# Five weight narrowings that share their exponent work with ScalarE, and two instead of three projections in the first three steps

## The chip, the core and the metric

One NeuronCore of a Trainium2 chip runs the whole kernel in one launch. The metric is the device time of one execution in microseconds. Eight executions of the kernel before took 1217.54 to 1219.71 us, with a median of 1218.54 us.

## The reference

```python
X = np.fft.fft(x, axis=1)               # x: 8 x 3136 x 256, float32
X = np.fft.fft(X, axis=2)
y = X.real.astype(np.float32)
h = np.maximum(y @ w_in, 0.0)           # w_in: 256 x 1024
conv_out = sum(conv_w[k] * hp[:, k:k + S, :] for k in range(3))   # hp: h padded by one row on each side
gate = 1.0 / (1.0 + np.exp(-conv_out))
return (h * gate @ w_out).astype(np.float32)                      # w_out: 1024 x 256
```

The real part of a two-dimensional Fourier transform is projected from 256 to 1024 features and rectified. A convolution with three taps along the sequence gives the gate, and the gated h is projected back to 256 features. The three weights arrive as float64, so the kernel has to make float32 of them itself.

## The kernel before

**Transform.** The sequence transform is folded: VectorE (DVE) adds and subtracts mirrored rows of x (`fold_ops`, lines 158 to 187), TensorE (PE) multiplies the folded rows with cosine and sine tables (`units`), and the results are two tables per batch, `pt` (cosine part) and `qt` (sine part), with 128 features by 1569 frequencies. The feature transform is not applied to the data: TensorE multiplies it into w_in once (`blocks`, line 595), which gives G, so that `pt` and `qt` are projected to the 1024 features directly.

**Steps.** The main loop runs over 256 steps (b, c, f): 8 batches, 4 chunks c of some 386 frequencies, 8 groups f of 128 features. A chunk stands for frequencies k and their mirror images, so a step makes two halves of h from the same products: the front half is pa + pb and the back half is pa - pb, each then rectified, where pa is the product with `pt` and pb that with `qt`. Each step goes through these stages, in functions of the same names:

- `seed`: ScalarE (ACT) fills the PSUM bank pa with a rank-one term (line 641). For the first four steps (`first`) there is no seed, and `products` adds a one-row matmul, `pa<-er,left`.
- `products`: TensorE writes pb from `qt` and adds the product with `pt` to pa. In the steps that `triple` picks (here the first 20), it adds the product with `qt` to pa once more, so that pa holds the sum.
- `copies`: in a triple step ScalarE copies -2 pb to SBUF as nb (line 670) and rectifies the front half of h straight out of pa (line 672). In any other step it copies pb twice, once for each half (line 675).
- `combine`: VectorE makes the halves of h that are left, max(pa + nb, 0), with one custom instruction each (line 686): one in a triple step, two in any other.
- `first_tap` (ScalarE, line 692), `other_taps` (VectorE, two instructions at line 698), `sigmoid` (ScalarE, two halves, line 711), `gate` (GpSimd line 718 and VectorE line 719, half each), and `mm2`: TensorE multiplies g with w_out, 6 matmuls of 256 columns in most steps, and the finished tiles go through ScalarE to SBUF and by DMA to HBM.

**Narrowing.** A float64 weight is loaded as pairs of 32-bit words (`raw`, low word and high word). `narrow` makes float32 of a block of 512 values per partition with seven VectorE instructions: take the exponent bits (515), subtract 896 and clamp at zero (516), shift left by 23 (517), add the sign bit (518), mask the mantissa (520), join it with the low word (521), multiply by the power of two (522). In the loop there are five narrowings of this size: the last quarter of w_in in step 0, and the quarters of w_out in steps 2, 3, 5 and 7. The raw words of w_out lie in a buffer that the second half of the next batch's x takes over afterwards.

**Order.** The order on every engine is that of the program text, written by hand. Work beside the steps is put into `side` with `at(cycle, where, fn)`, and cycle t of the loop runs:

```python
if 0 <= t - 2 < n: sigmoid(steps[t - 2])
if t + 1 < n:
    products(steps[t + 1]); copies(steps[t + 1])
run("act")
if t < n: combine(steps[t])
run("dve")
...                                # seed of t + 2, first_tap of t, other_taps of t - 1, gate of t - 2
run("load")
if t >= LAG: mm2(steps[t - LAG])   # LAG is 3
run("pe")
```

At the end of cycles 0, 1 and 2, "pe" runs `blocks(1)`, `blocks(2)` and `blocks(3)`, which make the parts of G, together with `column`, which makes the seed's factors ge (ScalarE copies them, lines 595, 600 and 609). PSUM has two banks for pa, one for pb, one for `pd` and four for po. The tile `left` holds the factors of the one-row matmul in one row of its features 0 to 3, and from the last chunk of a batch on it holds leftover rows of the gated h.

Of the kernel before, what the change touches and what calls it, by code (L numbers as in the profile page):

```python
# [9 lines left out]
F32 = mybir.dt.float32  # L10
I32 = mybir.dt.int32
U32 = mybir.dt.uint32
AF = mybir.ActivationFunctionType
ALU = mybir.AluOpType
# [12 lines left out]

TRIPLE = 20  # L30
FIRST = 4
RC = 56
NQ = 8
# [5 lines left out]
def kernel(  # L39
# [10 lines left out]
    nc = tc.nc  # L50
    B, S, D = x.shape
    F = moe_w_in.shape[1]
    P = 128
# [9 lines left out]
    NF = F // P  # L63
# [6 lines left out]
    const = ctx.enter_context(tc.tile_pool(name="const", bufs=1))  # L70
# [19 lines left out]
    stt = nc.vector.scalar_tensor_tensor  # L90
    act = nc.scalar.activation

    def mm(o, l, r, start, stop):
        nc.tensor.matmul(o, l, r, start=start, stop=stop, skip_group_check=True)  # L94
# [12 lines left out]
    sg = const.tile([P, 2, 2], F32, name="sg")  # L107
# [3 lines left out]
    def load_ops(b, h, eng, other=None, held=False):  # L111


        def plain():
            t = xp.tile([P, 8, 2, D], F32, name="xh", tag="xh")
            xh[b, h] = t
            if held:

                nc.gpsimd.memset(t[0:1, 0, 0, 0:1], 0.0)
            eng.dma_start(out=t[0:NP, 0:4], in_=bass.AP(  # L120
                tensor=x.tensor, offset=x.offset + (b * S + 1 + 2 * h) * D,
                ap=[[HQ * D, NP], [Q4 * D, 4], [1, 2 * D]]))

        def zero():
            t = xh[b, h]
            for s0, n, r in ((0, 4, 0), (4, 3, 1), (7, 1, 0)):
                (other or eng).dma_start(out=t[NP:KR, s0:s0 + n], in_=bass.AP(
                    tensor=x.tensor, offset=x.offset + (b * S + r * Q4) * D,
                    ap=[[D, 1], [Q4 * D, n], [0, 2], [1, D]]))

        def mirrored(m):
            def f():
                nc.gpsimd.indirect_dma_start(  # L133
                    out=xh[b, h][0:NP, 7 - m].rearrange("p q d -> p (q d)"),
                    out_offset=None,
                    in_=bass.AP(tensor=x.tensor, offset=x.offset,
                                ap=[[2 * D, B * S // 2], [1, 2 * D]]),
                    in_offset=bass.IndirectOffsetOnAxis(ap=idx[0:NP, 0:1], axis=0),
                    element_offset=(b * S + (4 - m) * Q4 - HO + 2 * (1 - h)) * D)
            return f  # L140
        return [plain] + [zero] * h + [mirrored(m) for m in range(4)]
# [63 lines left out]
    PQ, eb, er = {}, {}, {}  # L205
    ed = edp.tile([B, (RC // 2 + 1) * RC], F32, name="ed")

    def table(k, st, q, cols):
        return tabs[st // 2][0:k, st, q, cols] if st < 2 else tabs[1][0:k, st - 2, q, cols]
# [55 lines left out]
    def product(o, w, st, q, cols, start, stop):  # L265

        def f(p):
            k = KR if q == HQ - 1 else NP
            mm(p[o], w(k, q), table(k, st, q, cols), start, stop)
        return f  # L270
# [232 lines left out]
    left = const.tile([P, NF, P], F32, name="left")  # L503
# [1 line left out]

    def narrow(dst, raw):

        ts = nc.vector.tensor_scalar  # L510
        lsl, lsr = ALU.logical_shift_left, ALU.logical_shift_right
        lo, hi = raw[:, :, :, 0], raw[:, :, :, 1]
        lof, d = lo.bitcast(F32), dst.bitcast(I32)

        ts(out=d, in0=hi, scalar1=20, scalar2=0x7FF, op0=lsr, op1=ALU.bitwise_and)
        ts(out=d, in0=d, scalar1=-896, scalar2=0, op0=ALU.add, op1=ALU.max)
        ts(out=d, in0=d, scalar1=23, scalar2=None, op0=lsl)
        stt(out=d, in0=hi, scalar=-0x80000000, in1=d, op0=ALU.bitwise_and, op1=ALU.bitwise_or)

        ts(out=hi, in0=hi, scalar1=0xFFFFF, scalar2=0x100000, op0=ALU.bitwise_and, op1=ALU.bitwise_or)  # L520
        stt(out=lof, in0=lo.bitcast(U32), scalar=2.0 ** -32, in1=hi, op0=ALU.mult, op1=ALU.add)
        stt(out=dst, in0=lof, scalar=2.0 ** -20, in1=dst, op0=ALU.mult, op1=ALU.mult)

    class Weight:

# [7 lines left out]
        def load(self, eng):  # L533
            if self.raw is None:
                eng.dma_start(out=self.dst, in_=self.src)
            else:
                eng.dma_start(out=self.raw.rearrange("p c n e -> p c (n e)"), in_=self.src)

        def narrow(self, c0, c1):
            if self.raw is not None:  # L540
                narrow(self.dst[:, c0:c1], self.raw[:, c0:c1])

    ident = gp.tile([3 * NF, 3 * NF], F32, name="ident", tag="g")
    make_identity(nc, ident)
# [16 lines left out]
    def raw_in(i):  # L561
        def f(sh):
            if i % 2 == 0:
                raws[i // 2] = wp.tile([P, 2, *sh[1:]], I32, name="raw", tag="w%d" % (i // 2))
            return raws[i // 2][:, i % 2]
        return f

    w_in = [Weight(w4[i], moe_w_in[:, i * N4:(i + 1) * N4].rearrange("(t p) n -> p t n", p=P), raw_in(i))
            for i in range(4)]
# [13 lines left out]
    G = const.tile([P, 2, F], F32, name="G")  # L583
# [3 lines left out]
    def blocks(i):  # L587


        w = w4[i]  # L590
        for g in range(2):
            p = spare()
            for t in range(2):
                mm(p[:, 0:N4], dm[:, t, g, :], w[:, t], t == 0, t == 1)
            nc.scalar.copy(out=G[:, g, i * N4:(i + 1) * N4], in_=p[:, 0:N4])
        if 2 * i < FIRST:
            p = spare()
            for t in range(2):
                mm(p[0:1, N4:2 * N4], dm[:, t, 1, P - 1:P], w[:, t], t == 0, t == 1)
            nc.scalar.copy(out=left[0:1, 2 * i:2 * i + 2].rearrange("p f i -> p (f i)"), in_=p[0:1, N4:2 * N4])  # L600
        if i > 1:
            column(i)
# [15 lines left out]
    hs, gs, pa, pb, po, nb = {}, {}, {}, {}, {}, {}  # L618
# [5 lines left out]
    def cut(s):  # L624
        b, c, f = s
        ch = chunks[c]
        return ch, ch.k1 - ch.k0, slice(f * P, (f + 1) * P)

    def first(s):

        return s[0:2] == (0, 0) and s[2] < FIRST
# [10 lines left out]

    def triple(s):

        return s[0] == 0 and s[1] * NF + s[2] < TRIPLE

    def row_of(s):
        hs[s] = hp.tile([P, HW], F32, name="h", tag="h")
# [4 lines left out]
    def products(s):  # L653
        b, c, f = s
        ch, n, fs = cut(s)
        pb[s] = psb.tile([P, 512], F32, name="pb", tag="pb")
        mm(pb[s][:, 0:n], G[0:P - 1, 1, fs], PQ[b][1][0:P - 1, ch.k0:ch.k1], True, True)
        mm(pa[s][:, 0:n], G[:, 0, fs], PQ[b][0][:, ch.k0:ch.k1], first(s), not triple(s))
        if first(s):
            mm(pa[s][:, 0:n], left[0:1, f, :], er[b][:, ch.k0:ch.k1], False, False)  # L660
        if triple(s):
            mm(pa[s][:, 0:n], G[0:P - 1, 1, fs], PQ[b][1][0:P - 1, ch.k0:ch.k1], False, True)

# [25 lines left out]
    def first_tap(s):  # L689
        n = chunks[s[1]].w - 2  # L690
        gs[s] = gp.tile([P, HW - 2], F32, name="g", tag="g")[:, 0:n]
        act(gs[s], hs[s][:, 0:n], AF.Copy, scale=cw[:, 0, s[2]:s[2] + 1])  # L692
# [7 lines left out]
    def shares(s):  # L700

        ch = chunks[s[1]]
        w = ch.w - 2
        n = ch.rest[0] if ch.last else w
        return slice(0, n // 2), slice(n // 2, n), slice(n, w)

    def sigmoid(s):

        v, p, r = shares(s)
        for c in (slice(p.start, r.stop), v):  # L710
            act(gs[s][:, c], gs[s][:, c], AF.Sigmoid)  # L711
# [54 lines left out]
    for i in range(4):  # L766
        for j, u in enumerate(odds):
            u.part(i)
            if i == 3:
                u.copy()  # L770
                u.fin()
                if j == 1:
                    row()
                    w_out = Weight(wout, moe_w_out.rearrange("(c p) o -> p c o", p=P),
                                   lambda sh: xp.tile(sh, I32, name="raw", tag="xh"))
# [18 lines left out]
    def at(cycle, where, fn):  # L794
        side.setdefault((cycle, where), []).append(fn)

    for i in (1, 2, 3):
        at(i - 1, "pe", lambda i=i: blocks(i))
    at(0, "dve", lambda: w_in[3].narrow(0, 2))
    for i in (0, 1):  # L800
        at(i, "pe", lambda i=i: column(i))
    for cycle, c in ((2, 0), (3, 2), (5, 4), (7, 6)):
        at(cycle, "dve", lambda c=c: w_out.narrow(c, c + 2))
    for j, fn in enumerate(load_ops(1, 1, nc.sync)):
        at(NF + 1 + j // 3, "load", fn)

# [24 lines left out]
    for b in range(1, B):  # L831
        begin, us, *_ = units(b)
        us = us[0:4] + us[5:]
        c0, n = ends[b], per * b - 3 - ends[b]
# [12 lines left out]
    for b in range(1, B):  # L847
        ops = fold_ops(b)
        c0, n = ends[b - 1], ends[b] - ends[b - 1]
# [12 lines left out]
    n = len(steps)  # L862
# [4 lines left out]
    for t in range(n + LAG):  # L867
        def run(where):
            for fn in side.get((t, where), []):
                fn()  # L870
        if 0 <= t - 2 < n:
            sigmoid(steps[t - 2])
        if t + 1 < n:
            products(steps[t + 1])
            copies(steps[t + 1])
        run("act")
        if t < n:
            combine(steps[t])
        run("dve")
        if t + 2 < n:  # L880
            seed(steps[t + 2])
        if t < n:
            first_tap(steps[t])
        if 0 <= t - 1 < n:
            other_taps(steps[t - 1])
        if 0 <= t - 2 < n:
            gate(steps[t - 2])
        run("load")
        if t >= LAG:
            mm2(steps[t - LAG])  # L890
        run("pe")
# [66 lines left out]
```

## Time and profile before

| | |
|---|---|
| median of 8 executions | 1218.54 us (1217.54 to 1219.71) |
| the profiled execution: its time | 1218.51 us |
| its span in the profile | 1216.7 us, 15448 instructions |
| PE busy | 1186.6 us (98%) |
| DVE busy | 1125.8 us (93%) |
| ACT busy | 878.4 us (72%) |
| POOL busy | 373.4 us (31%) |
| mean granted TensorE clock | 0.996 of full speed |

The time is 1.8 us longer than the span, because launch and end lie outside the profile. A busy PE does not mean that PE is at its peak: matmuls are pipelined, and their ends are modelled. Times in the profile's rows count from the start of the span. L698 is line 698 of the kernel. PEld stands for the load of a matmul's stationary operand, which runs ahead of the matmul. A float32 matmul appears as two records, so "x2" is one product. "out<-in" names the tiles that an instruction writes and reads. In a row of the timeline, the first number is the start, the second the length, and a bracket at the end holds the idle time before it and what ended it.

### The profile page before, as it was taken

To read this page: it belongs to the slowest core of one execution; us is meant where nothing else is said; L and a number is where in the kernel's file an instruction comes from. 1 tells how busy PE (TensorE), PEld (TensorE's weight loads), DVE (VectorE), ACT (ScalarE), POOL (GpSimd) and SP (SyncE) were. 2 spreads that over 40 slices of the span, in tenths; PEclk is the share of its full clock that TensorE was granted. 3 is DMA by queue.
4 is the path that set the end of the run, shared out by engine and by line. 5 is a ranking of instruction groups with operands and counts; after the bars stand their busy time and mean duration, and the time that the engine had idled before them with its cause. 6 is when DMAs were issued, how large, how long until landed. Compare 5 with 4: busy or idle time off the path is not lost.

```text
span 1216.7 us, 15448 instructions
## 1 busy us (share of the span) xinstructions
PE 1186.6 (98%) x4876; PEld 908.8 (75%) x4876; DVE 1125.8 (93%) x1696; ACT 878.4 (72%) x1832; POOL 373.4 (31%) x474
## 2 busy tenths in 40 slices
PE   5999999999999999999999999999999999999998
PEld 4676777777777777777777777777777777777776
DVE  7899999999999999998999999999998988899996
ACT  2467656776777777777776777777777777788884
POOL 5224524343233232424224242332222222222222
PEclk9999999999999999999999999999999999999999
DMA  9512243211121110302121020210001000110000
GB/s 225 192 8 80 81 49 100 68 53 41 40 87 51 60 46 1 106 26 73 34 73 60 5 80 27 89 45 26 27 1 53 31 26 27 46 33 27 26 27 31
DMA packets 70213, 66.30 MB, mean 54 GB/s; under 512 B 28123, under 2 KB 57827, under 8 KB 70131
## 3 DMA queue, kind: packets, MB, share of 16 engines
q1 hardware_dynamic: 64493, 52.18, 15.1%
q0 software_dynamic: 5120, 12.85, 3.5%
q8 instruction: 39, 0.64, 0.2%
q10 hardware_dynamic: 518, 0.28, 0.1%
q14 instruction: 43, 0.35, 0.1%
HBM read 39.53 MB, written 25.74 MB: 54 GB/s over the span
## 4 chain that ended last, share of the span: by engine, by line
PE 70%; DVE 20%; issue 4%; ACT 2%; DMA 1%; DVEq 0%; SPq 0%; ACTq 0%
PE po L94 44%; PE pb L94 10%; PE pa L94 10%; DVE g L698 7%; PE pd L94 6%; DVE h L686 3%; DVE g L719 3%; DVE xh L158 2%; ACT nb L675 1%; DVE xh L169 1%; DVE w L186 1%; DVE w L187 1%; DMA xh<-in_x_dram 0%; DVE xh L173 0%; ACT g L711 0%
## 5 line engine op out<-in xcount | busy, mean ns | idle before, releaser
L94 PE MATMUL po<-wout,g 128*128 128x256 f32 x3072 | 712.0, 382 | 9.3 <-DVE g L719 8.6
L94 PEld LDWEIGHTS po<-wout,g 128*128 128x128 f32 x3072 | 581.6, 190 | 161.8 <-DVE g L719 40.0
L698 DVE SCALAR_TENSOR_TENSOR g<-h,cw,g 128x770 f32<-128x770 f32 (+1 forms) x512 | 550.3, 1075 | 9.3 <-ACT g L692 0.2
L718 POOL TENSOR_TENSOR g<-g,h 128x385 f32<-128x385 f32 (+1 forms) x256 | 233.7, 913 | 769.2 <-ACT g L711 489.3
L711 ACT ACTIVATE g<-g 128x385 f32<-128x385 f32 (+2 forms) x512 | 244.1, 526 | 190.6 <-DVE g L698 188.2
L675 ACT ACTIVATE nb<-pb 128x386 f32<-128x386 f32 (+2 forms) x472 | 208.2, 494 | 84.9 <-PE pb L94 84.0
L686 DVE CUSTOM_DVE_ANT_0 h<-pa,nb 128x386 f32<-128x386 f32 (+2 forms) x492 | 255.8, 560 | 3.6 <-ACT h L672 3.6
L692 ACT ACTIVATE g<-h,cw 128x770 f32<-128x770 f32 (+1 forms) x256 | 243.3, 950 | 0.2 <-DVE h L686 0.2
L94 PE MATMUL pb<-qt,G 127*128 127x387 f32 (+2 forms) x512 | 212.7, 496 | 0.0
L94 PE MATMUL pa<-pt,G 128*128 128x387 f32 (+2 forms) x512 | 211.9, 494 | 0.0
L641 ACT ACTIVATE pa<-eb,ge 128x387 f32<-128x387 f32 (+2 forms) x252 | 151.5, 601 | 1.3 <-PE pa L94 0.7
L94 PEld LDWEIGHTS pa<-pt,G 128*128 128x128 f32 x512 | 96.9, 189 | 73.5 <-issue 18.2
L719 DVE TENSOR_TENSOR g<-g,h 128x385 f32<-128x385 f32 (+1 forms) x256 | 145.4, 568 | 0.9 <-ACT g L711 0.9
L94 PE MATMUL pd<-tab,w 98*128 98x196 f32 (+3 forms) x448 | 126.8, 374 | 0.0
L133 POOL DMA_INDIRECT xh<-in_x_dram,idx x64 | 106.0, 1657 | 13.4 <-issue 9.3
L94 PEld LDWEIGHTS pb<-qt,G 127*128 127x128 f32 x512 | 94.2, 190 | 17.9 <-issue 1.4
L94 PEld LDWEIGHTS pd<-tab,w 98*128 98x128 f32 (+1 forms) x448 | 84.8, 191 | 12.2
L738 ACT COPY os<-po 128x256 f32<-128x256 f32 x196 | 57.6, 394 | 8.5 <-PE po L94 4.6
L158 DVE TENSOR_TENSOR xh<-xh 98x1020 f32<-98x1020 f32 (+1 forms) x32 | 40.8, 1279 | 2.6 <-DMA xh<-in_x_dram,idx 2.6
L169 DVE TENSOR_TENSOR xh<-xh 98x1024 f32<-98x1024 f32 (+1 forms) x32 | 42.0, 1313 | 0.1
L188 POOL COPY w<-xh 98x4 f32<-98x4 f32 (+1 forms) x32 | 19.6, 613 | 25.8 <-DVE xh L169 14.8
L291 DVE TENSOR_TENSOR qt<-as,pd 128x197 f32<-128x197 f32 (+1 forms) x14 | 7.2, 518 | 20.3 <-ACT as L287 20.3
(114 smaller groups left out, 392.0 us busy)
## 6 DMA issues: line engine op xcount, KB each, us to landing
out_dram<-os SPq DMA_DIRECT2D x192, 128.0 KB
xh<-in_x_dram SPq DMA_DIRECT2D x16, 784.0 KB
eb<-ed SPq DMA_DIRECT2D x16, 193.5 KB
tab<-dft_seq_dram SPq DMA_DIRECT2D x4, 589.5 KB
raw<-in_moe_w_in_dram SPq DMA_DIRECT2D x4, 512.0 KB
raw<-in_moe_w_out_dram SPq DMA_DIRECT2D x1, 2048.0 KB
eb<-ed SPq DMA_DIRECT2D x8, 209.0 KB
eb<-ed SPq DMA_DIRECT2D x8, 193.0 KB
```

The costliest lines, as they stand in the source:

```text
L94: nc.tensor.matmul(o, l, r, start=start, stop=stop, skip_group_check=True)
L133: nc.gpsimd.indirect_dma_start(out=xh[b, h][0:NP, 7 - m].rearrange("p q d -> p (q d)"), out_offset=None, in_=bass.AP(tensor=x.tensor, offs ...
L158: vt(a[:, :, :, 1:D], a[:, :, :, 1:D], r[:, :, :, D - 1:0:-1], op=ALU.add)
L641: act(pa[s][:, 0:n], eb[b, c], AF.Copy, scale=ge[:, f:f + 1])
L675: act(nb[s][:, i, cols], p[:, cols], AF.Copy, scale=-1.0 if i else 1.0)
L686: nc.vector._custom_dve(TENSOR_ADD_SAT, out=to, in0=a[:, cols], in1=c[:, i, cols], s0=BIG, s1=0.0)
L692: act(gs[s], hs[s][:, 0:n], AF.Copy, scale=cw[:, 0, s[2]:s[2] + 1])
L698: stt(out=g, in0=h[:, k:k + n], scalar=cw[:, k, f:f + 1], in1=g, op0=ALU.mult, op1=ALU.add)
L711: act(gs[s][:, c], gs[s][:, c], AF.Sigmoid)
L718: gt(g[:, p], g[:, p], h[:, p], op=ALU.mult)
L719: vt(g[:, v], g[:, v], h[:, v], op=ALU.mult)
L738: nc.scalar.copy(out=osb[:, j % 2], in_=pt[:, j % 2])
```

## The change

- `narrow` now gives two parts, `power` and `product`. When it is given a spare buffer (`room`), ScalarE does the subtraction, the clamp and the shift in one ACTIVATE, `Relu(2^23 * d - 896 * 2^23)`, on the integer words in place, so that VectorE has five instructions instead of seven. The mantissa goes into `room` instead of back into raw, and the sign is added after the join.
- For the five narrowings in the loop, `power` is put at a new place, "first", in the cycle: after `sigmoid` and ahead of `products` and `copies`. `product` stays at "dve". The narrowings ahead of the loop keep their seven instructions.
- `room` is the upper half of `left` (features 4 to 7), which nothing else uses before the last chunk of the first batch.
- `triple` leaves out steps 0 to 2: they have no third product, two copies of pb, and two custom instructions in `combine`.
- One memset of a constant [128, 1] is added on GpSimd at the start.

```diff
-TRIPLE = 20
+TRIPLE = 3, 20
...
+    low = const.tile([P, 1], F32, name="low")
+    nc.gpsimd.memset(low, -896.0 * 2 ** 23)
+
+    def narrow(dst, raw, room=None):
...
+        sg = hi
+        if room is not None:
+            c, n = hi.shape[1:]
+            sg = room[:, 0:c * n].rearrange("p (c n) -> p c n", c=c)
+
+        def power():
+
+            ts(out=d, in0=hi, scalar1=20, scalar2=0x7FF, op0=lsr, op1=ALU.bitwise_and)
+            if room is not None:
+                act(d, d, AF.Relu, scale=2.0 ** 23, bias=low[0:d.shape[0]])
+            else:
+                ts(out=d, in0=d, scalar1=-896, scalar2=0, op0=ALU.add, op1=ALU.max)
+                ts(out=d, in0=d, scalar1=23, scalar2=None, op0=lsl)
+
+        def sign():
+            stt(out=d, in0=hi, scalar=-0x80000000, in1=d, op0=ALU.bitwise_and, op1=ALU.bitwise_or)
+
+        def product():
+
+            if room is None:
+                sign()
+            ts(out=sg, in0=hi, scalar1=0xFFFFF, scalar2=0x100000, op0=ALU.bitwise_and, op1=ALU.bitwise_or)
+            stt(out=lof, in0=lo.bitcast(U32), scalar=2.0 ** -32, in1=sg, op0=ALU.mult, op1=ALU.add)
+            if room is not None:
+                sign()
+            stt(out=dst, in0=lof, scalar=2.0 ** -20, in1=dst, op0=ALU.mult, op1=ALU.mult)
+        return power, product
...
-        return s[0] == 0 and s[1] * NF + s[2] < TRIPLE
+        return s[0] == 0 and TRIPLE[0] <= s[1] * NF + s[2] < TRIPLE[1]
...
-        mm(pa[s][:, 0:n], G[:, 0, fs], PQ[b][0][:, ch.k0:ch.k1], first(s), not triple(s))
+        mm(pa[s][:, 0:n], G[:, 0, fs], PQ[b][0][:, ch.k0:ch.k1], first(s), not first(s) and not triple(s))
         if first(s):
-            mm(pa[s][:, 0:n], left[0:1, f, :], er[b][:, ch.k0:ch.k1], False, False)
+            mm(pa[s][:, 0:n], left[0:1, f, :], er[b][:, ch.k0:ch.k1], False, not triple(s))
...
-    at(0, "dve", lambda: w_in[3].narrow(0, 2))
+
+    room = left[:, NF // 2:].rearrange("p f i -> p (f i)").bitcast(I32)
+
+    def shared(cycle, w, c):
+        for where, fn in zip(("first", "dve"), w.parts(c, c + 2, room)):
+            at(cycle, where, fn)
+
+    shared(0, w_in[3], 0)
...
     for cycle, c in ((2, 0), (3, 2), (5, 4), (7, 6)):
-        at(cycle, "dve", lambda c=c: w_out.narrow(c, c + 2))
+        shared(cycle, w_out, c)
...
         if 0 <= t - 2 < n:
             sigmoid(steps[t - 2])
+        run("first")
         if t + 1 < n:
             products(steps[t + 1])
             copies(steps[t + 1])
```

More of the change, by code (lines that the diff above doesn't have):

```diff
@@ L503 @@
     left = const.tile([P, NF, P], F32, name="left")
-    def narrow(dst, raw):
+    low = const.tile([P, 1], F32, name="low")
+    nc.gpsimd.memset(low, -896.0 * 2 ** 23)
+    def narrow(dst, raw, room=None):
         ts = nc.vector.tensor_scalar
@@ L513, in narrow @@
         lof, d = lo.bitcast(F32), dst.bitcast(I32)
[L515 to L522, printed above, removed]
+        sg = hi
[20 more added lines that the diff above has]
+        return power, product
     class Weight:
@@ L537, in load, with parts @@
                 eng.dma_start(out=self.raw.rearrange("p c n e -> p c (n e)"), in_=self.src)
+        def parts(self, c0, c1, room=None):
+            if self.raw is None:
+                return []
+            return narrow(self.dst[:, c0:c1], self.raw[:, c0:c1], room)
         def narrow(self, c0, c1):
-            if self.raw is not None:
-                narrow(self.dst[:, c0:c1], self.raw[:, c0:c1])
+            for f in self.parts(c0, c1):
+                f()
     ident = gp.tile([3 * NF, 3 * NF], F32, name="ident", tag="g")
```

## The prediction

> **What bounds the kernel now.** I read the page first, then the chain of waits by stretches of time, then the timeline of steps 0 to 8 (42 to 100 us). The page gives most of the chain to PE:
>
> ```profile
> ## 4 chain that ended last, share of the span: by engine, by line
> PE 70%; DVE 20%; issue 4%; ACT 2%; DMA 1%; DVEq 0%; SPq 0%; ACTq 0%
> ```
>
> The change lies in steps 0 to 7, so those 70% don't settle it. Busy time by stretches (columns: stretch, length, busy time and count for each engine, granted clock, DMA):
>
> ```profile
> 59.00:66.00 7.00, 7.00 (x31) 4.65 (x31) 6.76 (x12) 5.42 (x12) 1.27 (x2) 1.00 0.31 4
> 66.00:73.00 7.00, 7.00 (x26) 4.74 (x25) 6.86 (x9) 4.63 (x10) 2.08 (x3) 1.00 0.46 4
> 91.00:98.00 7.00, 4.60 (x13) 3.22 (x13) 6.93 (x10) 3.97 (x8) 1.29 (x2) 0.76 0.43 117
> 118.00:154.00 36.00, 34.84 (x141) 24.65 (x140) 35.72 (x47) 25.15 (x60) 17.23 (x16) 1.00 0.26 77
> ```
>
> DVE (third pair) is full from 59 us on. PE is full too until 91, then loses 2.4 us of 7. The chain agrees: PE carries it to 56.0, DVE from 56.6 to 147, DVE with PE and ACT by turns to about 289 us, then PE to the end. No piece of it after 97 us is a DMA. So what DVE gains or loses by step 8 is passed on to the end as a shift. The stretch that decides is step 2, where PE, ACT and DVE meet:
>
> ```profile
> 55.05 0.92 PE L94 MATMUL pa<-qt,G 127*128 127x386 f32 x2
> 55.80 1.89 PE L94 MATMUL po<-win,dm 128*128 128x256 f32 x8
> ...
> 56.59 0.56 DVE L686 CUSTOM_DVE_ANT_0 h<-pa,nb 128x385 f32<-128x385 f32 x1 [2.82 <-ACT h L672]
> ...
> 57.53 0.43 DVE L516 TENSOR_SCALAR wout<-wout 128x512 int32<-128x512 int32 x1
> ...
> 57.99 0.43 DVE L517 TENSOR_SCALAR wout<-wout 128x512 int32<-128x512 int32 x1
> 58.46 0.69 DVE L518 SCALAR_TENSOR_TENSOR wout<-raw,wout 128x512 int32<-128x512 int32 x1
> ...
> 59.41 0.16 ACT L609 COPY ge<-po 128x2 f32<-128x2 f32 x1 [0.73 <-PE po L94]
> 59.59 1.28 ACT L711 ACT_TABLE_LOAD   x1
> ...
> 60.88 0.94 ACT L711 ACTIVATE g<-g 128x385 f32<-128x385 f32 x2
> 60.98 1.02 DVE L698 SCALAR_TENSOR_TENSOR g<-h,cw,g 128x770 f32<-128x770 f32 x1
> ```
>
> DVE waits 2.82 us for the third product of step 2 and the rectification behind it, then narrows from 57.06 to 60.98. ACT copies ge, which ends `blocks(2)` and its columns on PE, then loads the sigmoid's table, then does sigmoid(0).
>
> **The third products.** Each of steps 0 to 2 loses one product with `qt`. Start to start it costs PE 0.75 (45.31 to 46.06), 0.76 (48.29 to 49.05) and 0.75 us (55.05 to 55.80): 2.26 us in all. PE has no idle matmul time from 43 to 91 us, so its rows from `blocks(2)` on move up by 2.26 us until something else is late. On ACT the number of copies stays at two per step. pb's single bank comes free one copy later (0.4 us), which PE covers with pa and the one-row product. DVE gets three more custom instructions at 0.47 us of pitch, 1.41 us, all ahead of the wait found next; without that cover they would cost those 1.41 us.
>
> **Two instructions less on DVE.** By starts, L516 to L518 is 57.53 to 58.46: 0.93 us for each narrowing, 4.65 for five. They count only where DVE is late.
>
> **The ACTIVATE.** The trace has none from int32 to int32. Nearest are L692 with 770 elements (0.93 us) and L641 with 387 (0.59); between them, 512 elements take 0.70 us. Lower bound: 0.5 us, as L672 for 385. Upper bound: 1.4, if integer words went at half the rate. I take 0.70, as both rows have a per-partition operand and float32 of the same width. The Trainium skill, "ScalarE: Activation LUTs", section "Rules for kernel authors", speaks against this: max and multiply belong on VectorE. By engine time the rows are 0.70 us against 0.93, and here DVE is the one that is late in steps 3 to 8 while ACT has 2 of 7 us free. Taken as a rule for the path (0.70 paid, nothing hidden), five would cost 3.5 us and eat the gain; by the rows it holds only where DVE waits for ACT.
>
> **Where DVE waits for ACT.** The ACTIVATE of step t stands behind sigmoid(t - 2) and ahead of the copies for t + 1. In step 0 it runs at 46.5 to 47.2 (DVE's first instruction needs 0.42 us after 46.02), and DVE is then busy with two custom instructions, the mask and the join, 2.1 us, before it needs the exponent. DVE then ends step 0's narrowing at about 49.9 instead of 51.3, and reaches the join of step 2 by about 55.8, 3 us ahead. There it needs the ACTIVATE, which is queued behind the ge copy, the table load and sigmoid(0). Those follow PE: the table load ends at 60.87 - 2.26 = 58.61, sigmoid(0) at 59.56, the ACTIVATE at 60.18. The sign starts at 60.22 and, with 0.72 + 0.61 to the next starts, other_taps at 61.55 instead of 60.98. The 0.5 us by which GpSimd's gate (61.56) stretches the second of them goes, since that gate now runs about 59.1 to 60.3. So gate(0) starts at 61.55 + 1.98 (as 68.85 to 70.83) = 63.53 us, before 63.46. All that DVE had gained, about 4 us, is waited away: step 2 gives -0.07. Behind the waiting sign stand other_taps(1) and gate(0), and PE's mm2(0); PE reaches mm2(0) at 68.59 - 2.26 = 66.33, so it isn't held. Behind the ACTIVATE on ACT stand copies(3), at 60.2 instead of 61.73, early enough for PE's pb of step 4 at 63.4.
>
> **Steps 3, 5 and 7.** other_taps end, then sigmoid (0.94) and the ACTIVATE (0.70), 1.65 us; on DVE meanwhile gate 0.47, exponent 0.45, custom 0.47, mask 0.46, join 0.72, 2.57 us. So 0.9 us of cover, no wait, and 0.93 us gained each time: 2.79 us. Copies come 0.6 us later on ACT, in a place where it waited 0.74 (step 3) to 0.87 us for PE. Step 4's and 6's parts don't change. gate(5) starts 2.79 - 0.07 = 2.7 us earlier.
>
> **PE at step 8.** The row that closes the stretch:
>
> ```profile
> 94.04 4.54 PE L94 MATMUL po<-wout,g 128*128 128x256 f32 x12 [2.40 <-DVE g L719]
> ```
>
> PE is ready for mm2(5) about 2 us earlier and DVE 2.7, so it starts at 91.3 and about 1.5 to 2 us of idle stay. The row takes 4.54 instead of 2.75 us because the granted clock fell (0.76 in 91 to 98). "TensorE: Matmul & The Clock Gate", section "What's actually happening", asks for about 3.4 us of idle before the clock halves; this trace halves it after 2.4 us. By the page the shorter gap would never cost the 1.8 us, by the row it may. Either way the sum is the same: from 118 to 153 us DVE is the late one and absorbs it.
>
> **Moved or added at nothing.** The memset is some 0.1 us on GpSimd at the start. No DMA is moved in the text; the next half of x is issued when the last narrowing is done (91.55), so 2.7 us earlier, and is needed at 124. w_out's packets had landed by 42 us, so the first instruction of step 2 at about 53 finds its data. The mask that now writes to `room` has the same size and kind (0.43).
>
> Sum: 1218.51 - 2.7 = 1215.8 us; the profiled execution lies 0.03 us under the median, so this is the figure for the median too. What the six stretches by GpSimd between 60 and 95 us (0.45 to 1.4 each) do is open: if the three that hit narrowings (0.55, 0.54, 0.51) vanish, 1214.2; if three more come, 1217.4.
>
> **Rivals.**
> - *The wait in step 2 is shorter than I think* (ACT's order as it runs lets the ACTIVATE come earlier, or GpSimd collides less). DVE could at most keep its 4 us: 1218.5 - 2.7 - 3.9 = 1211.9; half of it, 1213.8. For it: no row shows ACT in the new order. Against: an engine's rows here run in the order of the text.
> - *Given back.* DVE is no longer the late engine somewhere in 97 to 289 us, or ACT's copies, now later, hold PE. For it: the chain there alternates with ACT and PE rows. Against: those are fed by DVE and shift with it. A third to all of the gain lost: 1217.5.
> - *Slower: the price of the integer ACTIVATE.* Call it p. In step 2 every us over 0.70 is paid at once, and in steps 3, 5, 7 every us over 1.6. The gain is gone at 2.7 = (p - 0.7) + 3(p - 1.6), p = 2.05 us. At 3.3 us it would be -2.7 + 2.6 + 5.1 = +5.0: 1223.5. For it: no such row in the trace. Against: it is three times any row of its size.
> - *The two edits don't act where they are put:* DVE would then show L516 and L517 still, and no change at all, 1218.5. The order of the built program shows 10 DVE instructions less in the loop's narrowings and 3 more custom ones, so I give it nothing.
>
> **Chances.** My forecast 0.50 (1214.8 to 1216.8; three fifths of it below 1216.1), shorter wait 0.20, given back 0.22, slower 0.08. A measurement of this kernel can tell about 0.2% (2.4 us) from no change, and the forecast is near that line: faster 0.32 + 0.20 + 0.02 = 0.54, same 0.18 + 0.20 = 0.38, slower 0.08. The range 1213.3 to 1218.2 leaves out the full 3.9 us, the last of the given-back cases and the slower one, some 0.2.
>
> **What would show it.** Right: in step 2 a DVE idle of about 4 us ahead of the sign, released by the ACTIVATE at L527 at about 60.2; PE's `blocks(2)` at 53.5; gate(0) near 63.5; gate(5) near 90.7 instead of 93.43; PE's wait for mm2(5) under 2.4 us; the same distance of 2.7 us still at 150 and 290 us. Wrong: an ACTIVATE over 1 us, a DVE idle before the sign in steps 3, 5 or 7, PE idle before 91 us, or a distance that shrinks between 97 and 289 us.

## The result, and the profile after

The changed kernel takes 1214.47 us (median of 11 runs, 1213.43 to 1215.52), the kernel before in the same series 1218.35 us (31 runs). The ratio is 0.9967, 95% interval 0.9960 to 0.9975: 3.9 us less. The prediction was 1215.8 us with a range of 1213.3 to 1218.2, so the direction and the range held; the gain was 3.9 instead of 2.7 us.

The profiled execution of the changed kernel took 1214.9 us, its span is 1213.1. The page's chain and busy times hardly differ from before:

```profile
PE 1184.4 (98%) x4870; PEld 907.7 (75%) x4870; DVE 1119.9 (92%) x1689; ACT 881.3 (73%) x1837; POOL 373.3 (31%) x475
...
PE 71%; DVE 20%; issue 4%; ACT 2%; DMA 1%; DVEq 0%; SPq 0%; ACTq 0%
```

DVE has 5.9 us less to do and the end comes 3.6 us sooner in this pair of profiles. The stretches say more (busy times in the order PE, PEld, DVE, ACT, POOL, then clock, DMA share, GB/s):

```profile
59.00:66.00 7.00, 7.00 (x29) 4.48 (x28) 4.04 (x6) 6.34 (x13) 0.98 (x2) 1.00 0.38 5
...
91.00:98.00 7.00, 7.00 (x31) 5.57 (x30) 6.93 (x8) 5.14 (x10) 2.98 (x3) 1.00 0.23 62
```

From 59 to 66 us DVE is now idle for 3 of 7 us, where it was full, and ACT is nearly full. From 91 to 98 PE has no gap any more and keeps its clock. This is step 2 of the changed kernel in the timeline (the profile's line numbers have moved: L533 sign, L539 mask, L540 join, L543 product, L713 custom, L725 other_taps, L746 gate, L738 sigmoid, L527 the new ACTIVATE):

```profile
55.12 1.99 PE L94 MATMUL po<-win,dm 128*128 128x256 f32 x8
55.36 1.03 DVE L713 CUSTOM_DVE_ANT_0 h<-pa,nb 128x385 f32<-128x385 f32 x2 [1.02 <-PE pa L94]
...
56.75 0.69 DVE L540 SCALAR_TENSOR_TENSOR raw<-raw,left 128x512 f32<-128x512 uint32 x1
...
59.01 1.28 ACT L738 ACT_TABLE_LOAD   x1
...
60.30 0.94 ACT L738 ACTIVATE g<-g 128x385 f32<-128x385 f32 x2
...
61.15 0.71 ACT L527 ACTIVATE wout<-wout,low 128x512 int32<-128x512 int32 x1
...
61.89 0.69 DVE L533 SCALAR_TENSOR_TENSOR wout<-raw,wout 128x512 int32<-128x512 int32 x1 [4.44 <-ACT wout L527]
```

DVE has joined the mantissa at 57.4 and waits 4.44 us for the ACTIVATE, which stands behind the table load and sigmoid(0), as forecast. And this is the place where PE waited for DVE before:

```profile
90.09 0.82 PE L94 MATMUL pa<-qt,G 127*128 127x387 f32 x2
90.74 2.75 PE L94 MATMUL po<-wout,g 128*128 128x256 f32 x12
```

mm2(5) follows the product before it after 0.65 us, the pitch of a product, so there is no wait.

**A common clock for the comparisons.** Profiles of these kernels start the loop at different times: the first product `pb<-qt,G` of step 0 starts at 42.97 us in the profile of before and at 44.34 in that of after. The cause lies ahead of the loop: in the changed kernel's trace PE's clock rises 22.1 us ahead of that product, in that of before 23.6 (PE makes 4 records of the folded products per us before that moment and 6 after it). The runs below have values from 22.1 to 23.5 that don't go with their edits, so I count from that product. The second thing is one row of the profile of before: other_taps in step 6 took 3.49 us there (82.67), and 2.55 in the run with warm-up products below (e4), whose instructions are the same up to step 8. So e4 serves as the base. (It was luck that the profile of before, on whose 1218.51 us the prediction built its sum, still lay at the median: its way from the first folded product to the loop, 27.3 us, is the shortest of all traces, and that and its long other_taps cancel.) Starts of DVE's gate(s) against it, each counted from the first product of its own trace:

| run | gate(0) | gate(1) | gate(3) | gate(5) | end of the trace | median against before |
|---|---|---|---|---|---|---|
| changed kernel | +0.40 | -1.06 | -2.62 | -4.10 | -3.83 | -3.9 |
| e1 products alone | -2.13 | -2.11 | -2.11 | -2.12 | -1.82 | -1.8 |
| e2 ScalarE alone | +2.34 | +0.88 | -0.68 | -2.16 | -1.96 | -2.0 |
| e3 step 2 early | -3.55 | -1.92 | -3.12 | -4.44 | -4.23 | -3.7 |
| e5 behind combine | +1.63 | +0.51 | -0.33 | -1.17 | -0.96 | -1.1 |
| e6 DVE alone, head | -3.34 | -2.89 | -3.22 | -3.64 | -3.41 | -3.3 |
| e7 steps 2 and 3 early | -3.55 | -3.32 | -3.58 | -4.65 | -5.04 | -5.4 |
| e8 ACTIVATE twice | +0.40 | -1.07 | -2.62 | -4.08 | -3.81 | -4.2 |
| e9 all early | -3.55 | -3.32 | -3.85 | -4.69 | -5.10 | -4.6 |
| e10 ScalarE in 5 and 7 | -3.33 | -2.90 | -3.58 | -4.66 | -5.05 | -4.8 |

In every row the distance at gate(5), step 7, is that at the end within 0.45 us, and the medians, which come from other executions, follow within 0.6. The rows show how each narrowing adds to it. Most of what changes after gate(5) changes between gate(9) and gate(10), where VectorE's gate and GpSimd's overlap (e7 below).

### The profile page after: what moved, and what is told of

The parts are those of the page before. It is cut to its first block, busy times and chain, and to the rows that moved or that the text cites. A ratio compares the mean times of both kernels' runs of the same rounds, so it can differ in the third digit from the quotient of the medians.

```text
span 1213.1 us, 15439 instructions
## 1 busy us (share of the span) xinstructions
PE 1184.4 (98%) x4870; PEld 907.7 (75%) x4870; DVE 1119.9 (92%) x1689; ACT 881.3 (73%) x1837; POOL 373.3 (31%) x475
## 4 chain that ended last, share of the span: by engine, by line
PE 71%; DVE 20%; issue 4%; ACT 2%; DMA 1%; DVEq 0%; SPq 0%; ACTq 0%
PE po L94 44%; PE pb L94 10%; PE pa L94 10%; DVE g L725 7%; PE pd L94 6%; DVE h L713 3%; DVE g L746 3%; DVE xh L158 2%; ACT nb L702 1%; DVE xh L169 1%; DVE w L186 1%; DVE w L187 1%; DMA xh<-in_x_dram 0%; ACT g L738 0%; DVE xh L173 0%
## 5 line engine op out<-in xcount | busy, mean ns | idle before, releaser
L725 DVE SCALAR_TENSOR_TENSOR g<-h,cw,g 128x770 f32<-128x770 f32 (+1 forms) x512 | 548.9, 1072 | 9.3 <-ACT g L719 0.2
L738 ACT ACTIVATE g<-g 128x385 f32<-128x385 f32 (+2 forms) x512 | 244.2, 526 | 190.2 <-DVE g L725 189.8
L702 ACT ACTIVATE nb<-pb 128x386 f32<-128x386 f32 (+2 forms) x478 | 210.8, 493 | 86.1 <-PE pb L94 85.0
L713 DVE CUSTOM_DVE_ANT_0 h<-pa,nb 128x386 f32<-128x386 f32 (+2 forms) x495 | 257.2, 560 | 1.0 <-PE pa L94 1.0
L746 DVE TENSOR_TENSOR g<-g,h 128x385 f32<-128x385 f32 (+1 forms) x256 | 146.3, 571 | 0.9 <-ACT g L738 0.9
```

The source lines that it names most:

```text
L702: act(nb[s][:, i, cols], p[:, cols], AF.Copy, scale=-1.0 if i else 1.0)
L713: nc.vector._custom_dve(TENSOR_ADD_SAT, out=to, in0=a[:, cols], in1=c[:, i, cols], s0=BIG, s1=0.0)
L725: stt(out=g, in0=h[:, k:k + n], scalar=cw[:, k, f:f + 1], in1=g, op0=ALU.mult, op1=ALU.add)
L746: vt(g[:, v], g[:, v], h[:, v], op=ALU.mult)
```

## The experiments

Theory A is the prediction's: how late DVE is by step 8 is handed on to the end. The rivals: the parts simply add up (C), PE bounds (B, D), the gain is the clock drop that went away (E); later, where a narrowing's gain comes from (F, G, H).

**e1, the products alone.** The kernel before with

```diff
-TRIPLE = 20
+TRIPLE = 3, 20
...
-        return s[0] == 0 and s[1] * NF + s[2] < TRIPLE
+        return s[0] == 0 and TRIPLE[0] <= s[1] * NF + s[2] < TRIPLE[1]
```

and the two lines for start and stop of the products.

> The kernel before with the third products of steps 0 to 2 left out, and all five narrowings on DVE. Theory A (DVE's lateness at step 8 is handed on to the end): nothing on DVE waits for ACT in step 2, so combine(2) starts about 1.9 us earlier after the start of the loop, and gate(0) about 2.6 us: 1218.35 - 2.6 = 1215.8 us, if GpSimd's collisions stay. Rival B (the products are worth what PE saves): 2.05 us, 1216.3. Rival C (the two parts add up and the collisions belong to neither): this and the run with ScalarE alone lie together 3.9 us under the kernel before.

1216.3 us, ratio 0.9984 (0.9975 to 0.9993). gate(0) comes 2.13 us earlier, and gate(9) still does. Rival B's 2.05 and theory A's 2.6 both lie within the interval; PE's own rows are 1.95 us earlier at mm2(0).

**e2, ScalarE alone.** The changed kernel with

```diff
-TRIPLE = 3, 20
+TRIPLE = 0, 20
```

> The changed kernel with the third product back in steps 0 to 2. Theory A: the ACTIVATE of step 2 follows the table load of the kernel before (60.87) and sigmoid(0), so it ends at 62.5, gate(0) comes 2.4 us later than before, and steps 3, 5 and 7 give back 3 x 0.93: about -0.4, 1218.0 us if the stretches by GpSimd stay, 1216.0 if the 2 us of them that the changed kernel's profile lacks belong to the ScalarE narrowing. Rival C (parts add up): 1217 or less, and a wait of DVE in step 2 that costs nothing.

1216.1 us, 0.9986 (0.9977 to 0.9995). The first figure of A is right, +2.34 us at gate(0); after that each narrowing gives 1.46 to 1.56 us, not 0.93. With e1 it adds up to -3.8 us, so C's sum holds, but not its wait that costs nothing: DVE waits 4.24 us for the ACTIVATE in step 2, and gate(0) comes late for it. It isn't two savings, though: step 2 alone loses 2.34 us here and gains 2.13 in e1, and in the changed kernel the two come to +0.40, because the products on PE set when the table load, and with it the ACTIVATE, can come.

**e3, the ACTIVATE of step 2 earlier.** In the changed kernel:

```diff
-        for where, fn in zip(("first", "dve"), w.parts(c, c + 2, room)):
-            at(cycle, where, fn)
+        power, product = w.parts(c, c + 2, room)
+        if cycle == 2:
+            at(1, "load", power)
+        else:
+            at(cycle, "first", power)
+        at(cycle, "dve", product)
```

> The changed kernel with the ACTIVATE of step 2 (and its first DVE instruction, whose place on DVE stays the same) put at the end of step 1, ahead of the copies of G, the table load and sigmoid(0). Theory A: the 4.4 us wait of DVE goes, gate(0) comes up to 3.9 us earlier and is then held by sigmoid(0); PE waits less from step 9 on, where it still waited some 7 us in all: 1211.5 us (1210.6 to 1212.5). Rival D (PE bounds steps 3 to 8 in the changed kernel, the wait of step 2 costs nothing): 1214.5.

1214.38 us, 0.9965 (0.9951 to 0.9979), no measurable gain on the changed kernel. Theory A's figure missed and rival D's fits, and in both traces mm2(0) to mm2(8) start at the same times, so PE has no gap in these steps that an earlier DVE could fill. But the wait in step 2 didn't cost nothing: it is gone, gate(0) is 3.95 us earlier than in the changed kernel, and the wait came back one narrowing later. (That PE's rows don't set the end shows in e7.) The timeline of e3:

```profile
65.92 0.16 ACT L636 COPY ge<-po 128x2 f32<-128x2 f32 x1 [0.41 <-PE po L94]
65.98 0.94 ACT L738 ACTIVATE g<-g 128x385 f32<-128x385 f32 x2
...
66.82 0.71 ACT L527 ACTIVATE wout<-wout,low 128x512 int32<-128x512 int32 x1
...
67.56 0.69 DVE L533 SCALAR_TENSOR_TENSOR wout<-raw,wout 128x512 int32<-128x512 int32 x1 [2.80 <-ACT wout L527]
```

In step 3 the ACTIVATE stands behind the ge copy that ends `blocks(3)` on PE. DVE being early only makes it wait 2.80 us there. Of 3.95 us, 0.86 are left at gate(1) and 0.34 at gate(5).

**e4, keeping PE warm.** In the kernel before:

```diff
+        if t == 8:
+            warm = psd.tile([P, 512], F32, name="pd", tag="pd")
+            for _ in range(8):
+                mm(warm[:, 0:2 * P], G[:, 0, 0:P], G[:, 0, 0:2 * P], True, True)
```

> The kernel before with eight products of 128 x 256 more (1.7 us of PE, never read) ahead of mm2(5), so that PE does not idle there and its clock stays up. Theory A: PE's lost 1.8 us are absorbed by DVE, which is late from 118 us on: no change, 1218.4. Rival E (the gain beyond my 2.7 us is the clock drop at 94 us that the changed kernel doesn't have): 1216.6.

1218.0 us, 0.9997 (0.9988 to 1.0006): no change. I had mis-sized the addition (16 records at 0.216 us are 3.5 us, twice what I wrote), and mm2(5) came 0.9 us later than in the profile of before. The clock stayed up all the same:

```profile
91.00:98.00 7.00, 7.00 (x32) 5.66 (x31) 6.93 (x10) 3.97 (x8) 1.22 (x2) 1.00 0.39 119
```

Neither the 1.8 us of clock that PE got back nor the 0.9 us that it lost reach the end. The record says the same of the kernel before as it is: of its 54 executions in the series of e1 to e10, 26 had a mean granted clock of 1.000, which leaves no room for the 1.7 us that the drop at 94 us took (0.0014 of the span), and their median is 1218.7 us against 1217.8 for the others. So executions without the drop are no faster. And the changed kernel's trace has one of its own (0.57 of full speed from 206 to 210 us) that e8's lacks, and both end within 0.03 us of each other. Rival E falls.

**e5, not at the head of the step.**

```diff
-        for where, fn in zip(("first", "dve"), w.parts(c, c + 2, room)):
-            at(cycle, where, fn)
+        for fn in w.parts(c, c + 2, room):
+            at(cycle, "dve", fn)
```

> The changed kernel with the first part of the five narrowings no longer at the head of the step: on DVE the exponent comes behind the custom instructions, on ScalarE the ACTIVATE comes behind the copies. Theory F (what each narrowing in steps 3, 5 and 7 gained over my 0.93 us, 0.55 us, comes from the place: GpSimd's gate now falls on the custom instruction, which doesn't mind it, and not on a tensor_scalar): the stretches of about 0.5 us come back in the narrowing's instructions, and DVE waits some 1 us each for an ACTIVATE behind copies that wait for PE: 1217.5. Rival G (the place is indifferent, five instead of seven instructions is all): 1214.5.

1217.04 us, 0.9990 (0.9981 to 0.9999). The place, for both engines together, is worth 2.6 us. Of the 2.93 us between its gate(5) and the changed kernel's, 1.23 are from step 2, where the ACTIVATE now also stands behind the copies (DVE waits 5.33 us). The other 1.70 are from steps 3, 5 and 7 (0.34, 0.72 and 0.64). There the exponent takes 1.00, 0.94 and 0.93 us instead of 0.42, and the sign waits 0.28 and 0.23 us in steps 5 and 7. The stretches came back as F had it; the waits were a quarter of what it had.

**e6, no ACTIVATE at all.** As in the changed kernel, but with L516's and L517's work kept on DVE behind the custom instructions:

```diff
-                act(d, d, AF.Relu, scale=2.0 ** 23, bias=low[0:d.shape[0]])
...
+                return
...
+            if room is not None:
+                shift()
```

(`shift` holds the two tensor_scalar instructions.)

> No ACTIVATE: all seven instructions of a narrowing on DVE, but the first of them at the head of the step ahead of the custom instructions; third products of steps 0 to 2 left out, as in the run with the products alone (1216.3). Theory F: three stretches of 0.5 us go and in step 2 the exponent fills DVE's wait for PE (0.4 us): 1214.4. Rival G: 1215.9.

1214.79 us, 0.9971 (0.9961 to 0.9982). This cannot be told from the changed kernel: without any help from ScalarE nearly the same time. The figure is F's, but not by F's sum. GpSimd's stretches didn't go, they moved: L524 took 0.89 us in step 7, L544 1.33 in step 5, L547 1.38 in step 3. Against e1, 1.21 of 1.53 us are there at the start of gate(0): the exponent fills DVE's wait for PE in step 2, no stretch falls on other_taps(1) (2.07 instead of 2.56), and some instructions follow others at a shorter distance (below). But that stretch has moved too, onto gate(0) itself:

```profile
60.44 1.23 DVE L750 TENSOR_TENSOR g<-g,h 128x385 f32<-128x385 f32 x1
```

It takes 0.55 us in e1, so 0.78 us are left at gate(1); the rest is gained in steps 5 and 7 (0.33 and 0.42).

**e7, steps 2 and 3 early.** As e3, with `if cycle in (2, 3): at(cycle - 1, "load", power)`.

> The changed kernel with the first part of the narrowings of steps 2 and 3 put at the end of the step before, ahead of ScalarE's copies of G. With step 2 alone moved, the wait came back in step 3 (2.8 us). Theory A (DVE's lateness at step 8 is handed on): that wait goes too, gate(5) comes 2.5 us earlier than in the changed kernel: 1212.0. Rival D (PE bounds now, its waits later are for something else): 1214.4.

1212.69 us, 0.9952 (0.9938 to 0.9965), the lowest median, though the runs of e9 and e10 overlap with its own. Its five runs (1212.32 to 1213.26) all lie below the changed kernel's eleven, so D's 1214.4 is out. gate(1) is 2.26 us earlier than in the changed kernel, but gate(5) only 0.55: DVE now waits 0.79 us in step 3 and 1.13 us in step 5 for ACTIVATEs.

So theory A, which wanted 2.5 us at gate(5), explains less than half of the 1.21 us that are there at the end of the trace. Another 0.62 come at gate(9), far from any narrowing. In the changed kernel

```profile
107.65 2.25 DVE L746 TENSOR_TENSOR g<-g,h 128x385 f32<-128x385 f32 x1
107.79 1.68 POOL L745 TENSOR_TENSOR g<-g,h 128x385 f32<-128x385 f32 x2
```

and in e7

```profile
106.71 1.42 DVE L746 TENSOR_TENSOR g<-g,h 128x385 f32<-128x385 f32 x1
106.85 2.00 POOL L745 TENSOR_TENSOR g<-g,h 128x385 f32<-128x385 f32 x2
```

In the changed kernel DVE's half of gate(9) ends only after two of GpSimd's halves, in e7 before the second of them. It takes 2.25 us in the changed kernel, e1 to e3, e5, e6 and e8, and 1.42 or 1.43 in the kernel before, e4, e7, e9 and e10. What decides it was not tried, so this part of e7's gain can't be credited to the earlier ACTIVATEs.

**e8, the ACTIVATE twice** in steps 3, 5 and 7:

```diff
...
+        if cycle in (3, 5, 7):
+            d = w.dst[:, c:c + 2].bitcast(I32)
+            at(cycle, "first", lambda: act(d, d, AF.Copy))
```

> The changed kernel with a second ACTIVATE (a copy of the same 512 words onto themselves) behind the ACTIVATE of steps 3, 5 and 7. My prediction's cover of 0.9 us: ScalarE's 0.6 us more are hidden in all three steps, 1214.5. Rival (ScalarE's time is on the path there, as the rule that multiply belongs on VectorE would have it): 0.6 us for each, 1216.3.

1213.98 us, 0.9965 (0.9951 to 0.9979). Three more ACTIVATEs of 0.63 us leave every gate of the table within 0.02 us of the changed kernel's. The cover is there.

**e9, all four early.** `at(cycle - 1, "load", power)` for every cycle but 0.

> The changed kernel with the first part of the narrowings of steps 2, 3, 5 and 7 all put at the end of the step before. With steps 2 and 3 alone moved it took 1212.7, with waits of DVE for the ACTIVATE of 0.8 us in step 3 and 1.1 us in step 5. Theory A: the wait in step 5 goes, gate(5) comes 1 us earlier: 1211.7. Rival: sigmoid, which now stands behind one more ACTIVATE that waits for DVE, makes gate and GpSimd late, or PE bounds from here on: 1212.7 or more.

1213.37 us, 0.9956 (0.9943 to 0.9970): A's figure missed, and the rival's (1212.7 or more) holds. The wait in step 5 shrank to 0.30 us, but GpSimd's gate, which comes later behind the later sigmoid, now hits the product (L543, 1.24 us) and the sign (L533, 1.36).

**e10, ScalarE only where it isn't held.** e6 for steps 0, 2 and 3, the changed kernel for steps 5 and 7.

> The exponents on ScalarE in steps 5 and 7 only; in steps 0, 2 and 3 all seven instructions stay on DVE, the first of them at the head of the step, as in the run without any ACTIVATE (1214.8). Theory H (ScalarE's share is worth some 1.2 us in each step in which ScalarE doesn't stand behind PE's blocks, and nothing or less in step 2, where DVE waits 4.4 us for it): 1214.8 - 2.3 = 1212.5. Rival (the changed kernel's gain is one from the place and the products alone, ScalarE adds nothing anywhere): 1214.8. Rival (PE bounds by then): 1213.5.

1213.24 us, 0.9959 (0.9945 to 0.9972). Between H's 1212.5 and the rival's 1213.5. In step 7 the shared narrowing gives 1.08 us (0.42 in e6), in step 5 only 0.68 (0.33 in e6), since

```profile
75.41 0.69 DVE L536 SCALAR_TENSOR_TENSOR wout<-raw,wout 128x512 int32<-128x512 int32 x1 [0.98 <-ACT wout L533]
```

DVE waits again (line numbers of e10: L536 is the sign, L533 the ACTIVATE). Of the 1.6 us between the ends of e10's and e6's traces, 0.62 are gate(9)'s, as in e7. In e7, e9 and e10 gate(5) lies within 0.05 us, and PE runs without a gap up to mm2(9): its rows start at the same times in all three. Up to mm2(8) they do so in the changed kernel, e3 and e8 too, so an earlier DVE has nothing more to give to PE there. That PE's products are what holds ACT, and through it DVE, was read from ACT's waits and not tried by itself.

## Why the prediction was right, and where its sum was off

- *What bounds.* Right. The distance hardly changes from gate(11) on (-3.83 there, -3.81 at gate(50), -3.82 at gate(200) for the changed kernel): nothing later adds or takes. Between gate(9) and gate(10) 0.28 us are lost against e4, and 0.13 against the profile of before, which the prediction did not have.
- *Third products.* Mis-sized a little: 2.26 us forecast, 1.95 measured at mm2(0) in all runs without them but e5, where mm2(0) waits for DVE. In step 0 before,

```profile
45.31 0.92 PE L94 MATMUL pa<-qt,G 127*128 127x386 f32 x2
46.06 0.81 PE L94 MATMUL pb<-qt,G 127*128 127x386 f32 x2
46.71 0.81 PE L94 MATMUL pa<-pt,G 128*128 128x386 f32 x2
```

and after

```profile
46.67 0.92 PE L94 MATMUL pb<-qt,G 127*128 127x386 f32 x2
47.43 0.81 PE L94 MATMUL pa<-pt,G 128*128 128x386 f32 x2
```

What follows the one-row product is slower by 0.11 us to the next start. Before, that was the third product (0.75 us); now it is the next pb (0.76 instead of 0.65), in steps 1 and 2 the first products of `blocks`. So each third product was worth 0.65 us, not 0.75.
- *The wait in step 2.* Right in place and order: forecast about 4 us, sign at 60.22; measured 4.44 us, sign at 61.89 - 1.37 (the later start) = 60.52. gate(0) was forecast 0.07 us later, measured 0.40: PE's rows, which the table load follows, came 0.31 us less early than forecast.
- *The ACTIVATE's price.* 0.70 forecast, 0.71 measured. The rival that made it dear is out, and so is the rule cited in the prediction, as a rule for the path in steps 3, 5 and 7 (e8). In step 2, where DVE waits for ACT, every us of ScalarE counts.
- *Steps 3, 5 and 7: the step that failed.* I wrote "0.93 us gained each time: 2.79 us". Measured: 1.46, 1.56 and 1.48 us (differences of the first row of the table), 4.5 us. The mechanism was right and the size wrong, because I took away two instructions and left the pitch of the other five as it was. In step 7, DVE of e1 (seven instructions):

```profile
82.81 0.55 DVE L719 TENSOR_TENSOR g<-g,h 128x385 f32<-128x385 f32 x1
83.28 0.55 DVE L686 CUSTOM_DVE_ANT_0 h<-pa,nb 128x385 f32<-128x385 f32 x1
83.75 0.93 DVE L515 TENSOR_SCALAR wout<-raw 128x512 int32<-128x512 int32 x1
84.71 0.43 DVE L516 TENSOR_SCALAR wout<-wout 128x512 int32<-128x512 int32 x1
...
88.16 2.07 DVE L698 SCALAR_TENSOR_TENSOR g<-h,cw,g 128x770 f32<-128x770 f32 x2
```

and DVE of the changed kernel:

```profile
83.87 0.55 DVE L746 TENSOR_TENSOR g<-g,h 128x385 f32<-128x385 f32 x1
84.34 0.42 DVE L525 TENSOR_SCALAR wout<-raw 128x512 int32<-128x512 int32 x1
84.68 0.55 DVE L713 CUSTOM_DVE_ANT_0 h<-pa,nb 128x385 f32<-128x385 f32 x1
85.15 0.62 DVE L539 TENSOR_SCALAR left<-raw 128x512 int32<-128x512 int32 x1
85.81 0.69 DVE L540 SCALAR_TENSOR_TENSOR raw<-raw,left 128x512 f32<-128x512 uint32 x1
86.42 0.68 DVE L533 SCALAR_TENSOR_TENSOR wout<-raw,wout 128x512 int32<-128x512 int32 x1
...
87.74 2.07 DVE L725 SCALAR_TENSOR_TENSOR g<-h,cw,g 128x770 f32<-128x770 f32 x2
```

From gate to other_taps this is 5.35 against 3.87 us, 1.48 less. By starts: two instructions less, 0.93; the exponent 0.34 to the next start instead of 0.96, +0.62; the mask 0.66 instead of 0.46, -0.20; the join 0.61 instead of 0.73, +0.12; the sign 0.71 instead of 0.72. Two causes share the 0.55 over my figure. First, GpSimd's half of gate:

```profile
83.53 0.87 POOL L718 TENSOR_TENSOR g<-g,h 128x385 f32<-128x385 f32 x1 [1.46 <-PE pb L94]
```

in e1, and in the changed kernel

```profile
84.59 0.90 POOL L745 TENSOR_TENSOR g<-g,h 128x385 f32<-128x385 f32 x1 [1.46 <-ACT g L738]
```

In e1 it holds back the exponent until 84.4 (0.93 instead of 0.42 us). In the changed kernel it begins while the exponent is already running, which keeps its 0.42 us, and lies over the custom instruction, which takes its usual 0.55 us; only the end of it touches the mask (0.62 instead of 0.43). The Trainium skill ("SBUF — State Buffer", section "Who interferes with whom") has the rule behind it: GpSimd and VectorE share one pair of ports. A tensor_scalar can run in a mode that takes this pair too, and then whoever issues first keeps it for the whole instruction; a VectorE instruction outside these modes with at most one input from SBUF (the custom one reads pa from PSUM) doesn't contend. The rows agree; which mode an instruction ran in they don't say. e5, which undoes the place, has the exponent at 0.93 to 1.00 us again. Second, the start-to-start time is 0.10 to 0.12 us shorter where the next instruction doesn't read the result of the one before, which the new order makes true of exponent and custom, and of join and sign. In step 7 the first is worth 0.31 us (0.51 less on the exponent, 0.20 more on the mask), the second 0.24. The prediction had left the first open, as a term of up to 1.6 us in its range; the second it did not have. So the sum at gate(5) is 4.50 - 0.40 = 4.10 us instead of 2.79 - 0.07 = 2.7.

- *PE at step 8.* I forecast that 1.5 to 2 us of idle stay; none stayed. Counted from the first product, gate(5) came 5.07 us earlier than in the profile of before (0.97 of it for the long other_taps there), the product ahead of mm2(5) 2.11. That this would not matter, nor the clock, was right (e4).
- *ScalarE's part of the gain.* Not what the change's five ACTIVATEs suggest: e6 has none and is as fast. In step 2 they cost DVE its lead, in steps 3, 5 and 7 they earn it back. With the wait moved out of steps 2 and 3 (e7), the median is 2.1 us below that of e6; 1.0 us of this is made by gate(5), and 0.6 at gate(9) with an open cause.

## What to carry to other kernels

Work handed to another engine comes back at that engine's place in its own queue: look for what stands in front of it there, here a table load that waits for a third engine. An earlier engine gains only as far as the next such place, so the gain of one wait removed may be lost in the next (e3), and two must go together (e7). And when instructions are taken from a chain, count the starts, not the durations: what falls on GpSimd's work, and what waits for the result just before it, changes with the order. Last, a collision of 0.8 us far behind the change (gate(9)) can come or go with it, so a distance should be followed past the edited steps before it is credited to them.

## What the runs showed that I had not expected

- The start of the loop varies by 1.5 us between executions with the moment at which PE's clock rises: the first folded product starts 27.3 to 28.9 us ahead of the loop's first product, and the clock rises 3.7 to 6.8 us after it, also between kernels with the same text there. This is over a third of what this change is worth.
- One and the same instruction, other_taps in step 6, took 3.49 us in one execution and 2.55 in another with the same order of work ahead of it, next to four memsets and a gate on GpSimd.
- A distance of 3.83 us at gate(11) was still 3.82 us at gate(200), over 860 us and three engines that take turns in the chain.
